# A spectral filter and a two-layer MLP in one kernel: the second inverse result is passed on through DRAM, with new planning costs

## The chip, the cores and the metric

One core of one Trainium2 chip runs the whole kernel. The metric is the device time of one execution in microseconds (us), of which a median over runs is shown. Engines are called as in the profile: PE (TensorE's matrix products), PEld (its weight loads), DVE (VectorE), ACT (ScalarE), POOL (GpSimd) and SP (SyncE, which issues every DMA of this kernel).

## What is computed

The reference, cut to its two halves (8 sequences of 3136 tokens with 256 channels):

```python
X = np.fft.rfft(x, axis=1)                       # along the tokens
y = np.fft.irfft(X * (filt_r + 1j * filt_i), n=3136, axis=1)
mixed = np.real(np.fft.fft(np.fft.fft(y, axis=1), axis=2))
u = y + mixed
un = (u - mean(u)) / sqrt(var(u) + 1e-6)         # over the channels
out = u + maximum(un @ w_ch1, 0) @ w_ch2         # 256 -> 1024 -> 256
```

## The kernel before, in words

**Stages of one sequence (batch b).** Every transform is a product with a constant matrix, each number split in two halves of 16 bits, so that three products replace one in 32 bits. `first` (L541) makes the first step of the transform from `x` and stores it to a DRAM tensor `d1` (L551); `load_at` brings it back in another order as seven tiles `at` (L574); `spectrum` (L615) makes the second step and multiplies with the filter on DVE and POOL; a transposing DMA gives `z` (L660); `inverse1` (L729) goes back one step and stores to the DRAM tensor `d2` (L743); `load_b2` brings that back as tiles `b2` (L772); `inverse2` (L791) makes the last step, and ACT puts its result into tiles `ys` (L804). One `ys` tile holds 224 token pairs: 2 halves of 56 partitions, 4 columns j, 256 channels.

**From `ys` to the MLP.** The MLP works on groups g of 256 token pairs (49 groups in all), in tiles `y_g` of 128 partitions by 2 halves t by 2 kinds. A `ys` tile does not fall on such tiles: `place` (L751 to L762) cuts it at the borders and copies each piece from SBUF to SBUF (L761), 632 DMAs in all. `prepare` waits until all pieces of its group have been placed, mixes the channels on PE (L851), adds on DVE (L861), and takes the mean and variance (L939, L940, ACT L943). `normalize` then makes `un` (ACT L968), the upper half `u16` (ACT L973) and the lower one (POOL L979), and transposes them with a DMA into `ut` (L982), two of them per group. There are two `ut` buffers and five `y` buffers.

**The MLP.** `products` goes through steps q: step 8g+f computes block f of the first product of group g (L1004, six matmuls from `ut`), and two steps later its part of the second product (L1047, twelve matmuls from `h`, into two PSUM tiles `acc`, one per half t). Between them `rectify` takes `h` out of PSUM on ACT (L1033) and DVE (L1035). After block 7, `finish` adds the sums to `y` on DVE (L1061) and `store` writes the rows out (L1067).

**What sets the order.** Nothing in the order is made at run time. `Plan` plays all tasks through with one queue per engine; a task names an engine and a length (`yield "PE", 1.31`), and the instructions are written down in the order in which the plan serves them. Each engine executes its list in that order and waits at each instruction for its semaphores. `gate(t)` lets a task begin only after step t has been planned; `FIRST` is the step, relative to 8g, at which `prepare(g)` may begin, and `COME` the one for `inverse2`. For SP the plan used one hold per issue, whatever the transfer:

```python
if e == "SP":
    self.free_at[e] = self.now + ISSUE
    self.moved = max(self.moved, self.now + ISSUE + REACH) + length
    self.end = self.moved + LANDED
```

`free_at` is when SP can issue again, `moved` when the DMA engines will have moved the bytes, `end` when a reader may start.

The functions that the diff touches follow, with the line numbers of the profile.

Of the kernel before, what the change touches and what calls it, by code (L numbers as in the profile page):

```python
# [10 lines left out]
F32 = mybir.dt.float32  # L11
# [15 lines left out]
NS = N // 2  # L27
# [2 lines left out]
EXPO = 0x7F800000  # L30
LAG = 2
YBUFS = 5
FIRST = -11
COME = 15
PIECE = 1.15
HALF = 1.45
# [2 lines left out]
POOL_SPLITS = (2,)  # L39
RAW_IN = ("ys", "ys", "b2", "ut", "ut", "ys", "b2", "ys")  # L40
RAW_AFTER = (6, 7, 8, 9, 10, 17, 18, 15)
ISSUE = 0.45
REACH = 0.8
LANDED = 1.5
HOP = 0.4

# [11 lines left out]
class Plan:  # L58
# [75 lines left out]
    def run(self):  # L134
        while self.heap:
            self.now, _, f, args = heapq.heappop(self.heap)
            f(*args)
            while self.heap and self.heap[0][0] <= self.now:
                _, _, f, args = heapq.heappop(self.heap)
                f(*args)  # L140
            for e, queue in self.queues.items():
                if queue and self.free_at[e] <= self.now:
                    _, _, task, length = heapq.heappop(queue)
                    if e == "SP":
                        self.free_at[e] = self.now + ISSUE
                        self.moved = max(self.moved, self.now + ISSUE + REACH) + length
                        self.end = self.moved + LANDED
                    else:
                        self.end = self.free_at[e] = self.now + length
                    self.post(self.free_at[e], int)  # L150
                    self.step(task, None, self.free_at[e] if e == "SP" else None)
        assert not self.live
# [141 lines left out]
def _program(ctx, tc, nc, a, NB):  # L294
# [188 lines left out]
    def load_x(b, t):  # L483
        yield gate(t)
        if b == 1:
            yield until(("placed", 0, 1, 1))
        ms[b] = tp.tile([112, 8], F32, tag="mx", name=f"mx_{b}")
        for q in range(7):
            yield gate(t + 1.2 * q)
            yield until(("own", "x", b, q))  # L490
            yield "SP", 1.6, t + 1.2 * q
            nc.sync.dma_start(xs[b, q], a["x"][b, :, 4 * q : 4 * q + 4])
            done("x", b, q)
# [18 lines left out]
    def first(b, q, t):  # L512
# [23 lines left out]
            give("big", 21 * b + q // 2)  # L536
        kp = yield take("psf")
        p = bank(f"s1_{b}_{q}")[:112].rearrange("p (n c) -> p n c", c=256)
        yield "PE", 0.74
        for i, (hs, hx) in enumerate(((0, 0), (0, 1), (1, 0))):  # L540
            nc.tensor.matmul(p, s1[:, hs], x16[:, hx], start=i == 0, stop=i == 2)  # L541
        give("x16", k)
# [175 lines left out]
    def inverse1(b, ch, h, t):  # L718
# [8 lines left out]
        yield "PE", 0.74  # L727
# [17 lines left out]
        done("d2", b, ch, h)  # L745

    backs = {}

    y_at = {}

    def place(ys, r, n, j, kind, slot):  # L751

        while n:
            tile_, p = divmod(slot, 128)
            m = min(n, 128 - p)
            g = tile_ // 2
            if g not in ys_of:
                y_at[g] = yield take("y")
                ys_of[g] = mp.tile([128, 2, 2, 256], F32, tag="y", name=f"y_{g}", bufs=YBUFS)
            yield "SP", 0.2  # L760
            nc.sync.dma_start(ys_of[g][p : p + m, tile_ % 2, kind], ys[r : r + m, j])  # L761
            r, n, slot = r + m, n - m, slot + m  # L762

    def load_b2(b):
        yield until(*(("d2", b, ch, h) for ch in range(7) for h in range(2)))
# [36 lines left out]
    def bring(b, c, o, ys, ky, kp, p):  # L802
        yield "ACT", 0.63
        nc.scalar.activation(ys[:, 2 * o : 2 * o + 2], p, AF.Copy, scale=alphas[b][:, 2:3])  # L804
        give("psf", kp)
        if o:
            yield until(("placed", b, c, 0))
        for j in (2 * o, 2 * o + 1):
            slot = b * NS + 224 * c + 56 * j
            for h in range(2):  # L810
                if c or j:
                    yield from place(ys, 64 * h, 56, j, h, slot)
                else:
                    for kind in range(2):
                        yield from place(ys, 64 * h + 28 * kind, 28, j, kind, slot + 28 * h)
        done("placed", b, c, o)
        if o:
            give("ys", ky)


    total = NB * NS
# [7 lines left out]
    def gate(t):  # L829
        return until(("step", int(t))) if t >= 0 else until()  # L830
# [55 lines left out]
    def pieces(g, size):  # L886
        lo, hi = 256 * g, 256 * g + 256
        return [
            (b, c) for b in range(NB) for c in range(NS // size)
            if b * NS + size * c < hi and b * NS + size * c + size > lo  # L890
        ]

    def prepare(g):
        yield gate(8 * g + FIRST)
        yield until(*(("eo", b, c) for b, c in pieces(g, 224)), *((("i2",),) if g == 0 else ()))
        yield until(*(("placed", b, c // 2, c % 2) for b, c in pieces(g, 112)))
        tiles = [(256 * g + 128 * t, 256 * g + 128 * t + 128) for t in range(2)]
        y = ys_of.pop(g)
        fix = None
# [90 lines left out]
    def products():  # L990
        yield until(("w1",))
        for q in range(8 * ng + LAG):
            g, f = divmod(q, 8)
            if g < ng:
                yield until(("ut", g, 0), ("ut", g, 1))
                kp = yield take("psh")
                p = spare(f"h_{g}_{f}")
                yield "PE", 1.31, q
# [17 lines left out]
            if q >= LAG:  # L1016
                g, f = divmod(q - LAG, 8)
                yield until(("h", g, f), *((("w2",),) if q == LAG else ()))
                if f == 0:
                    accs[g] = []  # L1020
                    for t in range(2):
                        k = yield take("pso")
                        accs[g].append((k, ps_o.tile([128, 2, 256], F32, tag="pso", name=f"acc_{g}_{t}")))
                yield "PE", 1.32, q + 0.5
                second_product(g, f)
                if f == 7:
                    plan.spawn(finish(g), q - 1000)

    def rectify(g, f, p, kp):
        k = yield take("h")  # L1030
# [6 lines left out]
        hs[g, f] = k, h  # L1037
        done("h", g, f)

    def second_product(g, f):  # L1040
        k, h = hs.pop((g, f))
        c0 = 0
        for t in range(2):
            acc = accs[g][t][1]
            for kind in range(2):
                for i, (hh, hw) in enumerate(((0, 0), (0, 1), (1, 0))):
                    nc.tensor.matmul(  # L1047
                        acc[:, kind],
                        h[:, hh, c0 : c0 + 128],
                        w2s[:, f, hw],  # L1050
                        start=f == 0 and kind == 0 and i == 0,
                        stop=f == 7 and kind == 1 and i == 2,
                    )
                c0 += 128
        give("h", k)

    def finish(g):
        y = ready[g][0]
        for t, (k, acc) in enumerate(accs.pop(g)):
            yield "DVE", 0.7  # L1060
            nc.vector.scalar_tensor_tensor(y[:, t], acc, beta, y[:, t], op0=ALU.mult, op1=ALU.add)  # L1061
            give("pso", k)
            plan.spawn(store(g, t, y), 8 * g + 14)

    def store(g, t, y):
        yield "SP", 0.8
# [121 lines left out]
    for b in range(NB):  # L1188
# [19 lines left out]
        plan.spawn(load_b2(b), brought(b, 0))  # L1208
        plan.spawn(inverse2(b), brought(b, 0))
    for g in range(ng):  # L1210
        plan.spawn(prepare(g), 8 * g + FIRST)
    plan.spawn(products(), 0)
    with tc.manual_schedule():
# [55 lines left out]
```

## Time and profile before

| | us |
|---|---|
| runs without profile (3) | 1633.46 median, 1633.34 to 1637.3 |
| the profiled execution | 1631.1 |
| its span, first to last instruction | 1629.3 |
| PE busy in the span | 1401.4 (86%) |
| DVE / ACT / POOL busy | 1125.9 / 779.1 / 541.6 |
| mean granted TensorE clock | 0.933 of full speed |
| share of the 16 DMA engines' time (queue q1) | 64.6% |

The busy time of PE contains matmuls that ran while the granted clock was halved, so it is no measure of work alone. The first 190 us of the span contain no MLP step: there batch 0 is transformed and the weights are split. SP's time is not counted as busy by the profile; how long an issue holds it stands in the view of one line's instructions.

### The profile page before, as it was taken

Reading aid. Unit: us, or ns where it says so; the run is one execution under the profiler, and the core shown is the slowest. Engines: PE = TensorE matmul, PEld = TensorE weight load, DVE = VectorE, ACT = ScalarE, POOL = GpSimd, SP = SyncE. Lnnn points to the kernel's source line nnn. Section 1 sums busy time; section 2 is a strip of 40 time slices with the busy share of each in tenths; the row PEclk is TensorE's granted clock in tenths of the full one; section 3 lists DMA queues with packets and bytes.
Section 4 is the critical chain, followed back from the end, with each engine's and each line's share of the span. In section 5 each row is a group of like instructions: output and inputs, shape, how many; then the busy total and the mean of one; then the engine's idle time right before and its main releaser. Section 6 shows DMA issues by size and latency. Waiting matters only on the chain.

```text
span 1629.3 us, 30652 instructions
## 1 busy us (share of the span) xinstructions
PE 1401.4 (86%) x11217; PEld 947.2 (58%) x11217; DVE 1125.9 (69%) x2409; ACT 779.1 (48%) x1450; POOL 541.6 (33%) x675
## 2 busy tenths in 40 slices
PE   3341799988899989999889998899898998999999
PEld 1240366655665556656566566666565665666666
DVE  6784977776668657677567867687666866654662
ACT  4452745463544634364454545464554634534432
POOL 4460166201850155311660047301760056301100
PEclk9555699998999989999999999999999999999999
DMA  7985497646885486837866487847886596533321
GB/s 212 219 209 163 110 194 166 179 127 158 174 184 136 123 189 156 190 103 165 160 152 186 114 178 157 194 135 164 158 171 155 142 182 145 150 87 83 87 74 45
DMA packets 412071, 247.48 MB, mean 152 GB/s; under 512 B 238832, under 2 KB 365856, under 8 KB 411920
## 3 DMA queue, kind: packets, MB, share of 16 engines
q1 hardware_dynamic: 411920, 245.52, 64.6%
q8 instruction: 88, 1.44, 0.4%
q14 instruction: 63, 0.52, 0.1%
HBM read 87.62 MB, written 77.07 MB: 101 GB/s over the span
## 4 chain that ended last, share of the span: by engine, by line
PE 32%; DMA 8%; DVE 5%; SPq 4%; POOL 4%; issue 2%; ACT 1%; DVEq 0%; ACTq 0%; POOLq 0%
PE h L1004 13%; PE acc L1047 13%; DMA b<-d 3%; SPq L761 2%; DMA ut<-u 2%; DVE y L861 2%; PE y L791 2%; SPq L574 1%; PE s L541 1%; DVE h L1035 1%; POOL y L656 1%; PE mix L851 1%; DMA x<-x 1%; DMA y<-ys 1%; DMA z<-y 1%
## 5 line engine op out<-in xcount | busy, mean ns | idle before, releaser
L1004 PE MATMUL h<-ut,w1s 128*128 128x512 f16 x2352 | 586.9, 386 | 51.8 <-DMA ut<-u 46.6
L1047 PE MATMUL acc<-w2s,h 128*128 128x256 f16 x4704 | 590.4, 276 | 16.8 <-DVE y L1061 16.8
L1047 PEld LDWEIGHTS <-h 128*128 128x128 f16 x4704 | 460.7, 99 | 158.3 <-issue 28.1
L1033 ACT ACTIVATE h<-h 128x512 f16<-128x512 f32 x392 | 233.1, 595 | 551.8 <-PE h L1004 547.1
L1035 DVE SCALAR_TENSOR_TENSOR h<-h,h 128x512 f16<-128x512 f32 x392 | 268.0, 684 | 264.4 <-ACT h L1033 263.2
L1004 PEld LDWEIGHTS <-w1s 128*128 128x128 f16 x2352 | 225.9, 99 | 266.1 <-issue 44.4
L979 POOL TENSOR_TENSOR u<-un,u 128x512 f16<-128x512 f32 x94 | 109.1, 1161 | 642.2 <-ACT u L973 546.6
L861 DVE SCALAR_TENSOR_TENSOR y<-mix,alpha,y 128x508 f32<-128x508 f32 (+1 forms) x368 | 162.1, 478 | 33.4 <-PE mix L851 15.7
L641 POOL TENSOR_TENSOR yt<-yt,t 128x224 f32<-128x224 f32 x105 | 70.0, 667 | 209.9 <-DVE yt L633 143.7
L968 ACT ACTIVATE un<-y,sb 128x256 f32<-128x256 f32 x196 | 111.3, 596 | 23.7 <-DVE sb L955 22.7
L656 POOL TENSOR_TENSOR y<-yt,y 128x448 f16<-128x448 f32 x105 | 108.5, 1036 | 34.5 <-ACT y L650 34.3
L541 PE MATMUL s<-x,s 112*112 112x512 f16 x336 | 98.9, 418 | 17.1 <-ACT x L530 8.8
L740 DVE TENSOR_TENSOR bt<-i,bt 112x512 f16<-112x512 f32 x112 | 75.3, 685 | 35.9 <-ACT bt L738 32.2
L384 DVE TENSOR_REDUCE mx<-x 112x1 f32<-112x1024 f32 x56 | 67.6, 1214 | 41.7 <-DMA x<-x 41.5
L729 PE MATMUL i<-z,i 112*112 112x256 f16 x224 | 66.1, 295 | 31.4 <-DMA z<-y 27.8
L738 ACT CAST bt<-i 112x512 f16<-112x512 f32 x112 | 64.6, 584 | 56.6 <-PE i L731 51.1
L532 DVE SCALAR_TENSOR_TENSOR x<-x,sx,x 112x512 f16<-112x512 f32 x111 | 86.5, 800 | 5.2 <-ACT x L530 5.1
L627 DVE TENSOR_TENSOR yt<-s,ft 128x448 f32<-128x448 f32 x112 | 69.0, 616 | 30.4 <-PE s L616 30.0
L615 PE MATMUL s<-s,at 112*128 112x56 f16 x896 | 65.5, 194 | 27.9 <-DMA at<-d 23.9
L791 PE MATMUL y<-b,i 112*64 112x512 f16 (+1 forms) x480 | 63.3, 387 | 30.3 <-DMA b<-d 30.3
L804 ACT ACTIVATE ys<-y,alpha 128x512 f32<-128x512 f32 x112 | 72.6, 685 | 33.9 <-PE y L791 20.6
L548 DVE TENSOR_TENSOR ast<-s,ast 112x512 f16<-112x512 f32 x112 | 75.0, 683 | 18.7 <-ACT ast L546 18.5
(130 smaller groups left out, 1620.8 us busy)
## 6 DMA issues: line engine op xcount, KB each, us to landing
x<-x SPq DMA_DIRECT2D x56, 448.0 KB
d<-ast SPq DMA_DIRECT2D x112, 224.0 KB
at<-d SPq DMA_DIRECT2D x56, 448.0 KB
d<-bt SPq DMA_DIRECT2D x112, 224.0 KB
b<-d SPq DMA_DIRECT2D x56, 448.0 KB
out<-y SPq DMA_DIRECT2D x98, 256.0 KB
y<-ys SPq DMA_DIRECT2D x268, 56.0 KB
raw<-w SPq DMA_DIRECT2D x8, 512.0 KB
```

The source lines that it names most:

```text
L532: nc.vector.scalar_tensor_tensor(x16[:, 1], x, sx[:112, 1:2], x16[:, 0], op0=ALU.mult, op1=ALU.subtract)
L541: nc.tensor.matmul(p, s1[:, hs], x16[:, hx], start=i == 0, stop=i == 2)
L656: nc.gpsimd.tensor_tensor(y16[:, :, 1, :112], ytv, y16[:, :, 0, :112], op=ALU.subtract)
L740: nc.vector.tensor_tensor(bt[:, :, 1], p, bt[:, :, 0], op=ALU.subtract)
L791: nc.tensor.matmul(p[64 * h : 64 * h + 64, js], i2[:, i_, h, i], bt[:, 2 * o + js.start : 2 * o + js.stop, h], start=i == 0, stop=i == 1,)
L861: nc.vector.scalar_tensor_tensor(out, p, al, y, op0=ALU.mult, op1=ALU.add)
L968: nc.scalar.activation(un[:, k], y[:, t, k], AF.Identity, bias=sb[:, i, 1:2], scale=sb[:, i, 3:4])
L979: nc.gpsimd.tensor_tensor(u16[:, :, :, 1], unv, u16[:, :, :, 0], op=ALU.subtract)
L1004: nc.tensor.matmul(p.rearrange("p (t k q) -> p t k q", t=2, k=2), w1s[:, d, hw, 128 * f : 128 * f + 128], utv[:, :, :, d, hx], start=i == ...
L1033: nc.scalar.activation(h[:, 0], p, AF.Relu)
L1035: nc.vector.scalar_tensor_tensor(h[:, 1], p, 0.0, h[:, 0], op0=ALU.max, op1=ALU.subtract)
L1047: nc.tensor.matmul(acc[:, kind], h[:, hh, c0 : c0 + 128], w2s[:, f, hw], start=f == 0 and kind == 0 and i == 0, stop=f == 7 and kind == 1 ...
```

## The change

Three things move together.

- `bring` no longer copies pieces to the `y` tiles. It stores each `ys` tile, when both of its halves are there, to a DRAM tensor `dy` of its batch with two DMAs of 56 partitions by 4 columns (six DMAs for the first tile of a batch). A new task `fetch(g)` loads the `y` tile of a group from `dy`, 128 rows per DMA (more, smaller ones where a batch ends inside a tile). `prepare` waits for `fetch`.
- The plan's costs: SP is held 1.4 us by a transposing DMA (`TURN`; those have the length 1.65) and 0.5 by any other, and it is held longer when the planned DMA work is more than 4.5 us ahead (`BACKLOG`). `REACH` falls from 0.8 to 0.5. Three PE lengths fall (0.74 to 0.66 for `first` and `inverse1`, 1.31 to 1.3 for the first product). `FIRST` is -13, and `fetch` may begin three steps before that.
- `second_product` and `finish` are served by half t, so that other PE work can be planned between the halves, and the sums of half 0 can be taken out before half 1 is computed.

```diff
-FIRST = -11
+FIRST = -13
-ISSUE = 0.45
-REACH = 0.8
+ISSUE = 0.5
+TURN = 1.4
+BACKLOG = 4.5
+REACH = 0.5
...
                     if e == "SP":
-                        self.free_at[e] = self.now + ISSUE
-                        self.moved = max(self.moved, self.now + ISSUE + REACH) + length
+                        issue = TURN if length == 1.65 else ISSUE
+                        self.moved = max(self.moved, self.now + issue + REACH) + length
+                        self.free_at[e] = max(self.now + issue, self.moved - BACKLOG)
...
     def load_x(b, t):
         if b == 1:
-            yield until(("placed", 0, 1, 1))
+            yield until(("placed", 0, 1))
...
+        done("ys", b, c, o)
         if o:
-            yield until(("placed", b, c, 0))
-        for j in (2 * o, 2 * o + 1):
-            slot = b * NS + 224 * c + 56 * j
+            yield until(("ys", b, c, 0))
+            if c == 0:
+                dys[b] = dp.tile([NS, 2, 256], F32, tag="dy", name=f"dy_{b}", bufs=3)
+            rows = dys[b][224 * c : 224 * c + 224].rearrange("(j q) k c -> k q j c", j=4)
             for h in range(2):
-                if c or j:
-                    yield from place(ys, 64 * h, 56, j, h, slot)
+                j = int(c == 0)
+                yield "SP", 0.7
+                nc.sync.dma_start(rows[h, :, j:], ys[64 * h : 64 * h + 56, j:])
...
+    def fetch(g):
+        yield gate(8 * g + FIRST - 3)
+        y_at[g] = yield take("y")
+        y = ys_of[g] = mp.tile([128, 2, 2, 256], F32, tag="y", name=f"y_{g}", bufs=YBUFS)
+        yield until(*(("placed", b, c) for b, c in pieces(g, 224)))
+        for t in range(2):
+            q, g1 = 256 * g + 128 * t, 256 * g + 128 * t + 128
+            while q < g1:
+                b = q // NS
+                e = min(g1, (b + 1) * NS)
+                p = q % 128
+                yield "SP", 1.6 * (e - q) / 256
+                nc.sync.dma_start(y[p : p + e - q, t], dys[b][q - b * NS : e - b * NS])
+                q = e
+        done("y", g)
...
-        yield until(*(("placed", b, c // 2, c % 2) for b, c in pieces(g, 112)))
+        yield until(("y", g))
...
-                if f == 0:
-                    accs[g] = []
-                    for t in range(2):
+                for t in range(2):
+                    if f == 0:
                         k = yield take("pso")
...
-                yield "PE", 1.32, q + 0.5
-                second_product(g, f)
-                if f == 7:
-                    plan.spawn(finish(g), q - 1000)
+                    yield "PE", 0.655, q + 0.5
+                    second_product(g, f, t)
+                    if f == 7:
+                        plan.spawn(finish(g, t), q - 1000)
```

**Where instructions move.** Three places, as the order of instructions lists them: the line of the program, the operation, what it writes and from what, and its size. Names end in a buffer number.

Before, on SP, between the two transposes of group 6; the first one stands four rows ahead of this piece. `y_7` and `y_8` are the tiles of later groups, `ast` is a tile of `first` of batch 2.

```order
L761 DMA y_8_3717<-ys_1_2_3663 8x256
L761 DMA y_8_3717<-ys_1_2_3663 48x256
L761 DMA y_8_3717<-ys_1_2_3663 8x256
L761 DMA y_8_3717<-ys_1_2_3663 56x256 x2
L551 DMA d1_2_3409<-ast_2_8_3746 112x1024
L761 DMA y_7_3671<-ys_1_1_3630 16x256
L761 DMA y_7_3671<-ys_1_1_3630 40x256
L761 DMA y_7_3671<-ys_1_1_3630 16x256
L761 DMA y_7_3671<-ys_1_1_3630 40x256
L761 DMA y_7_3671<-ys_1_1_3630 56x256 x2
L551 DMA d1_2_3409<-ast_2_9_3791 112x1024
L982 DMA_TRANSPOSE ut_6_3680<-u16_6_1_3776 128x8x128
```

Changed, the same place, with both transposes of group 6:

```order
L803 DMA dy_1_3284<-ys_1_1_3581 56x4x256 x2
L554 DMA d1_2_3360<-ast_2_6_3542 112x1024
L803 DMA dy_1_3284<-ys_1_2_3645 56x4x256 x2
L991 DMA_TRANSPOSE ut_6_3663<-u16_6_0_3694 128x8x128
L554 DMA d1_2_3360<-ast_2_7_3697 112x1024
L760 DMA b2_1_3_3734<-d2_1_1947 112x8x256
L825 DMA y_7_3416<-dy_1_3284 128x512 x2
L991 DMA_TRANSPOSE ut_6_3663<-u16_6_1_3730 128x8x128
```

Twelve copies and several stores between the two transposes have become two loads of `y_7`, one `b2` load and one store; the four stores of `ys` tiles stand ahead of both.

Before, on ACT, around the cast of the second half of group 9 (`u16_9_1`); `h16_8_k` is the rectified block k of the group ahead of it, so it counts the steps.

```order
L968 ACTIVATE un_9_1_4766<-y_9_3997,sb_9_4712 128x256
L1033 ACTIVATE h16_8_1_4785<-h_8_1_4770 128x512
L968 ACTIVATE un_9_1_4766<-y_9_3997,sb_9_4712 128x256
L650 CAST y16_2_106<-yt_2_3_4572 128x4x112
L738 CAST bt_2_2_0_4819<-i1_2_2_0_4784 112x2x256
L804 ACTIVATE ys_1_5_4786<-y_1_5_0_4811,alpha_1_1333 128x512
L973 CAST u16_9_1_4826<-un_9_1_4766 128x4x128
L738 CAST bt_2_2_1_4859<-i1_2_2_1_4824 112x2x256
L804 ACTIVATE ys_1_5_4786<-y_1_5_1_4855,alpha_1_1333 128x512
L650 CAST y16_3_107<-yt_2_3_4572 128x4x112
L650 CAST y16_0_104<-yt_2_4_4748 128x4x112
L1033 ACTIVATE h16_8_2_4885<-h_8_2_4847 128x512
```

Changed, the same cast:

```order
L1041 ACTIVATE h16_8_4_4831<-h_8_4_4809 128x512
L977 ACTIVATE un_9_0_4827<-y_9_4135,sb_9_4778 128x256
L982 CAST u16_9_0_4871<-un_9_0_4827 128x4x128
L741 CAST bt_2_2_1_4853<-i1_2_2_1_4839 112x2x256
L977 ACTIVATE un_9_1_4828<-y_9_4135,sb_9_4778 128x256 x2
L982 CAST u16_9_1_4907<-un_9_1_4828 128x4x128
L1041 ACTIVATE h16_8_5_4899<-h_8_5_4886 128x512
```

The cast stood between blocks 1 and 2 of group 8 and now stands between blocks 4 and 5, three steps nearer to the product that needs it.

Before, on SP, where batch 5 brings its `at` tiles; `b2_4_3` is an input of `inverse2` of batch 4.

```order
L574 DMA at_5_1_10715<-d1_5_10630 112x8x256
L574 DMA at_5_2_10768<-d1_5_10630 112x8x256
L574 DMA at_5_3_10971<-d1_5_10630 112x8x256
L574 DMA at_5_4_11017<-d1_5_10630 112x8x256
L772 DMA b2_4_3_11400<-d2_4_9191 112x8x256
L574 DMA at_5_5_11100<-d1_5_10630 112x8x256
```

Changed, the same place:

```order
L760 DMA b2_4_3_11169<-d2_4_9029 112x8x256
L577 DMA at_5_0_10524<-d1_5_10488 112x8x256
L577 DMA at_5_1_10552<-d1_5_10488 112x8x256
L577 DMA at_5_2_10595<-d1_5_10488 112x8x256
L577 DMA at_5_3_10824<-d1_5_10488 112x8x256
L577 DMA at_5_4_10846<-d1_5_10488 112x8x256
```

The load of `b2_4_3` has moved from behind five `at` loads to ahead of all of them.

## Rows read from the trace of the kernel before

**Rows 1.** Stretches: us, busy us of each engine (count), PE clock, DMA share, GB/s

```profile
204.00:1420.00 1216.00, 1114.40 (x9211) 757.79 (x9210) 872.03 (x1891) 600.08 (x1114) 452.75 (x574) 0.97 0.70 160
1420.00:1629.30 209.30, 201.31 (x1470) 134.55 (x1467) 106.90 (x243) 77.44 (x142) 18.50 (x16) 0.99 0.32 77
```

**Rows 2.** Waits of PE, 204 to 1420 us: who for whom, us in total, times, longest

```profile
PE h L1004 <- DMA ut<-u: 45.7, 13, 8.0
PE acc L1047 <- DVE y L1061: 16.8, 11, 5.0
PE i L729 <- DMA z<-y: 12.9, 7, 7.7
PE s L615 <- DMA at<-d: 12.2, 7, 5.2
PE y L791 <- DMA b<-d: 9.8, 8, 2.8
```

**Rows 3.** SP's holds by line: count, ns least/median/most, first and last start

```profile
L761 SPq DMA_DIRECT2D y<-ys x632: 532/746/1729, 129.4 to 1573.3; - x158
...
L982 SPq DMA_TRANSPOSE ut<-u x98: 1232/1283/4143, 181.5 to 1590.6; - x98
...
L1067 SPq DMA_DIRECT2D out<-y x98: 332/376/3047, 224.1 to 1626.1; - x98
```

**Rows 4.** Timeline of SP, group 6: start us, us held, line, operation, count

```profile
355.50 1.27 SPq L982 DMA_TRANSPOSE ut<-u  x1
...
357.93 4.24 SPq L761 DMA_DIRECT2D y<-ys  x6
...
362.79 4.32 SPq L761 DMA_DIRECT2D y<-ys  x6
...
367.79 1.32 SPq L982 DMA_TRANSPOSE ut<-u  x1
```

**Rows 5.** Timeline of POOL and PE, group 6; in brackets idle time and its end

```profile
354.85 1.16 POOL L979 TENSOR_TENSOR u<-un,u 128x512 f16<-128x512 f32 x1 [2.90 <-issue]
...
371.33 1.01 PE L1004 MATMUL h<-ut,w1s 128*128 128x512 f16 x2 [7.96 <-DMA ut<-u]
```

**Rows 6.** Stretch behind that wait: columns as in the first group

```profile
371.00:378.00 7.00, 6.67 (x24) 3.36 (x24) 2.89 (x8) 1.21 (x2) 0.00 (x0) 0.55 0.38 115
```

**Rows 7.** Timeline of POOL, SP and PE, group 11

```profile
511.18 1.15 POOL L979 TENSOR_TENSOR u<-un,u 128x512 f16<-128x512 f32 x1 [1.18 <-issue]
...
510.73 2.86 SPq L982 DMA_TRANSPOSE ut<-u  x2
...
516.98 1.46 PE L1004 MATMUL h<-ut,w1s 128*128 128x512 f16 x6
```

**Rows 8.** Timelines of DVE and PE, group 34: a wait for the sums

```profile
1233.55 1.22 DVE L384 TENSOR_REDUCE mx<-x 112x1 f32<-112x1024 f32 x1 [4.84 <-DMA x<-x]
...
1239.63 2.72 PE L1047 MATMUL acc<-w2s,h 128*128 128x256 f16 x12 [4.96 <-DVE y L1061]
```

**Rows 9.** Timelines of SP and PE before the first product

```profile
129.38 9.38 SPq L761 DMA_DIRECT2D y<-ys  x12
...
139.39 8.55 SPq L761 DMA_DIRECT2D y<-ys  x12
...
149.16 3.70 SPq L492 DMA_DIRECT2D x<-x  x7
...
163.93 0.37 PE L361 MATMUL pt_w<-ident,mw 128*1 128x128 f32 x1 [19.15 <-ACT mw L1138]
```

**Rows 10.** Chain that ended last: start us, us, what (DMA: issue to landing)

```profile
746.42 1.92 DMA y<-ys
757.22 3.47 DMA d<-ast
...
766.32 10.16 DMA b<-d
...
1061.78 4.11 DMA b<-d
```

**Rows 11.** Page, DMA queue: packets, MB, share of 16 engines' span

```profile
q1 hardware_dynamic: 411920, 245.52, 64.6%
```

More of the change, by code (lines that the diff above doesn't have):

```diff
@@ L538, in first @@
         p = bank(f"s1_{b}_{q}")[:112].rearrange("p (n c) -> p n c", c=256)
-        yield "PE", 0.74
+        yield "PE", 0.66
         for i, (hs, hx) in enumerate(((0, 0), (0, 1), (1, 0))):
@@ L726, in inverse1 @@
         p = bank(f"i1_{b}_{ch}_{h}")[:112].rearrange("p (j c) -> p j c", j=2)
-        yield "PE", 0.74
+        yield "PE", 0.66
         for i in range(2):
@@ L747, in _program @@
     backs = {}
[L749 to L762, printed above, removed]
     def load_b2(b):
@@ L805, in bring @@
         give("psf", kp)
+        done("ys", b, c, o)
         if o:
-            yield until(("placed", b, c, 0))
-        for j in (2 * o, 2 * o + 1):
-            slot = b * NS + 224 * c + 56 * j
+            yield until(("ys", b, c, 0))
+            if c == 0:
+                dys[b] = dp.tile([NS, 2, 256], F32, tag="dy", name=f"dy_{b}", bufs=3)
+            rows = dys[b][224 * c : 224 * c + 224].rearrange("(j q) k c -> k q j c", j=4)
             for h in range(2):
-                if c or j:
-                    yield from place(ys, 64 * h, 56, j, h, slot)
-                else:
+                j = int(c == 0)
+                yield "SP", 0.7
+                nc.sync.dma_start(rows[h, :, j:], ys[64 * h : 64 * h + 56, j:])
+                if c == 0:
                     for kind in range(2):
-                        yield from place(ys, 64 * h + 28 * kind, 28, j, kind, slot + 28 * h)
-        done("placed", b, c, o)
-        if o:
+                        yield "SP", 0.1
+                        nc.sync.dma_start(rows[kind, 28 * h : 28 * h + 28, 0], ys[64 * h + 28 * kind : 64 * h + 28 * kind + 28, 0])
             give("ys", ky)
+            done("placed", b, c)
+    dys, y_at = {}, {}
+    def fetch(g):
[13 more added lines that the diff above has]
+        done("y", g)
     total = NB * NS
@@ L997, in products @@
                 p = spare(f"h_{g}_{f}")
-                yield "PE", 1.31, q
+                yield "PE", 1.3, q
                 ut = ready[g][1]
@@ L1018, in products @@
                 yield until(("h", g, f), *((("w2",),) if q == LAG else ()))
-                if f == 0:
-                    accs[g] = []
-                    for t in range(2):
+                for t in range(2):
+                    if f == 0:
                         k = yield take("pso")
-                        accs[g].append((k, ps_o.tile([128, 2, 256], F32, tag="pso", name=f"acc_{g}_{t}")))
-                yield "PE", 1.32, q + 0.5
-                second_product(g, f)
-                if f == 7:
-                    plan.spawn(finish(g), q - 1000)
+                        accs[g, t] = k, ps_o.tile([128, 2, 256], F32, tag="pso", name=f"acc_{g}_{t}")
+                    yield "PE", 0.655, q + 0.5
+                    second_product(g, f, t)
+                    if f == 7:
+                        plan.spawn(finish(g, t), q - 1000)
     def rectify(g, f, p, kp):
@@ L1038, in rectify, with second_product, finish @@
         done("h", g, f)
[L1040 to L1057, printed above, removed]
-        y = ready[g][0]
[L1059 to L1063, printed above, removed]
+    def second_product(g, f, t):
+        k, h = hs[g, f]
+        acc = accs[g, t][1]
+        for kind in range(2):
+            c0 = 256 * t + 128 * kind
+            for i, (hh, hw) in enumerate(((0, 0), (0, 1), (1, 0))):
+                nc.tensor.matmul(
+                    acc[:, kind],
+                    h[:, hh, c0 : c0 + 128],
+                    w2s[:, f, hw],
+                    start=f == 0 and kind == 0 and i == 0,
+                    stop=f == 7 and kind == 1 and i == 2,
+                )
+        if t:
+            give("h", k)
+    def finish(g, t):
+        y = ready[g][0]
+        k, acc = accs.pop((g, t))
+        yield "DVE", 0.7
+        nc.vector.scalar_tensor_tensor(y[:, t], acc, beta, y[:, t], op0=ALU.mult, op1=ALU.add)
+        give("pso", k)
+        plan.spawn(store(g, t, y), 8 * g + 14)
     def store(g, t, y):
@@ L1210, in _program @@
     for g in range(ng):
+        plan.spawn(fetch(g), 8 * g + FIRST - 3)
         plan.spawn(prepare(g), 8 * g + FIRST)
```

## The prediction

> **What bounds the kernel now.** I read the stretches first, to see where PE is idle. From 204 to 1420 us PE is busy for 1114.40 of 1216 us and idle for 101.6; after 1420 only 8.0 are idle, so that end has nothing to give [rows 1]. The same row shows the second loss: a mean granted clock of 0.97. The rows at the lower of the two levels (1.2 against 2.4 GHz) lie behind waits: after the longest one, 8 us at 371, the clock of the next 7 us was 0.55, though PE was busy for 6.67 of them [rows 5, 6]. Three per cent of 1216 us are 36 us (30 to 43 by the rounding), or 0.35 us for each of the 101.6 idle ones. I price an idle microsecond of that stretch at 1.35.
>
> Next the waits say what ended the idle time: 45.7 us in 13 waits for `ut`, the transposed input of the first product; 16.8 for the sums that DVE must take out; 34.9 for the tiles `z`, `at` and `b` [rows 2]. None of these is PE's own work, so the question is why `ut` is late.
>
> The timeline answers it. In group 6 POOL finished the second `u` at 356.01 (354.85 + 1.16) [rows 5], and its transpose was issued at 367.79 [rows 4]: 11.8 us in which SP worked off what stood ahead, 8.56 of them holds of twelve `y` copies. The transpose took 3.54 us to the product (371.33 - 367.79). In group 11 POOL finished at 512.33, SP issued its second transpose within the 2.86 us that began at 510.73, and the product began at 516.98 without a wait [rows 7]. So the same chain meets its date when SP is free, and misses it when SP is not. SP is the resource in short supply, by its holds and not by the bytes: a `y` copy holds it 0.746 us, a transpose 1.283, while the plan booked 0.45 for either [rows 3].
>
> **The change part by part.**
>
> *SP's holds.* Removed: 632 copies x 0.746 = 471 us. Added: the order lists 144 stores (96 + 16 large, 32 small) and 104 loads. Neither exists before. Bounds: 0.376, the hold of a 256 KB store of `out`, and 0.746, the old copy, since the new stores also start on 56 partitions [rows 3]; 248 of them are 93 to 185 us. I take 0.376 for the loads, which have the shape of the `out` stores, and 0.746 for the stores: 39 + 107 = 146. SP gets 325 us back (286 to 378), 0.20 of the span.
>
> *Waits for `ut`.* The hold ahead of group 6's second transpose falls from twelve copies to two loads, a `b` load and one store. Against it speaks the order: the cast of group 9 moved three steps nearer to its product, and counted over groups 1 to 48 `prepare`'s mixing product stands 8.1 steps ahead of the first product, where it stood 8.9, in spite of the -13. The plan now books SP nearer to its true holds, so this lead is one that it can keep. I take three quarters of 45.7: 35 us (from 0 to 45.7; the loss side is a rival below).
>
> *Waits for the sums, 16.8.* Serving the halves apart lets `finish` of half 0 start earlier in the order. But the longest of these, 4.96 us, was DVE standing in front of an `x` load for 4.84 us, with `finish` queued behind it [rows 8]. That goes only if the load comes earlier. I take 6 (0 to 16.8).
>
> *Waits for `b`, 9.8, and for `at` and `z`, 25.1.* In batch 5 the `b2` load now stands ahead of seven `at` loads instead of behind five; one behind such loads took 10.16 us to land, one elsewhere 4.11 [rows 10]. The order shows this in four batches of seven. I take 3 for `b` and 4 for the others (0 to 12 together), since SP serves them too.
>
> *The clock.* 35 + 6 + 7 = 48 idle us, times 0.35: 17 us.
>
> *The start.* Before 164 us two runs of twelve copies hold SP for 9.38 and 8.55 us ahead of the seven `x` loads of batch 1 [rows 9]. Now eight stores stand there: 6.0 us at 0.746, so the loads can go 12 us earlier. On the other side the raw weights of the second product are loaded later in the new order, and PE waited 19.15 us for just those [rows 9]; but its transpose now stands behind nine blocks of `first` and three of the MLP. I take 8 (-5 to 12).
>
> *The detour.* A copy landed in 1.92 us; a store to DRAM took 3.47 and a load from it 4.11 to 10.16 [rows 10], so a tile comes 5.7 to 11.7 us later, and SP waits for the store before it issues the load: everything behind it in SP's list waits too, transposes included. Cover: `fetch` may start at step -16 and the mixing product stands at -8; a step is about 2.9 us (1.46 for a block of the first product [rows 7], as much for the second, which has as many columns), so 23 us. Without that cover the sum of DVE would stand still for each late tile. Bytes: 25.7 MB more on 245.52, 10.5%, which turns a DMA share of 0.70 into 0.77 in the main stretch [rows 1, 11]. I charge 8 us (0 to 40): a tenth on what is left of the waits for `at`, `z` and `b`, and a few late tiles.
>
> The shorter PE lengths and `REACH` only shape the order; no instruction of PE is added or dropped.
>
> **Sum.** 48 + 17 + 8 - 8 = 65 us off. Against the profiled execution's own time, 1631.1: 1566. The median of the runs shown is 1633.46, 2.4 above that execution; with the same distance I forecast **1568**.
>
> **A rule against this.** Where rows 4 show twelve holds of SP between a finished `u` and its transpose, the Trainium skill ("DMA: Bandwidth & Descriptors", "Issuing engines are not separate DMA queues") says that the time a sequencer spends on starting a DMA is usually small relative to the DMA itself. By that rule the 325 us would be worth next to nothing; this trace speaks against it, with 0.746 us of hold for a copy that lands in 1.92.
> The same page ("Anatomy of one DMA") warns of a "surprisingly long delay especially when the write target is HBM" before a DMA's completion is signalled. The trace agrees: 3.47 against 1.92 us [rows 10], and the price of the detour is worked out from those rows alone.
>
> **The rivals.**
>
> *A, the forecast:* `ut` waits mostly gone, 1568 (own range 1535 to 1600).
>
> *B, the DMA engines take over.* SP is freed, but the engines, at 0.70 on average, are full where a batch brings its `at` tiles. Waits for `at`, `z`, `b` (34.9) rise by 28, and only `ut` and the sums gain 41: net 13 x 1.35 = 18, start and detour cancel: 1615. For it: 10.16 us for one `b` load. Against it: the copies already moved half of those bytes.
>
> *C, slower: the lead is too short.* The chain from the mixing product to `ut` lost 0.9 step x 2.9 = 2.6 us of lead per group, and 13 groups of 48 have 7 steps or fewer (9 before). If SP's delay in front of the transposes falls by less than 2.6 us, for instance because SP now stands waiting for stores to land, the waits grow: 48 x 2.6 = 125 us of lost lead, of which I let half reach PE, as the rest had slack. 62 more and 13 saved elsewhere: 49 x 1.35 = 66: 1700. For it: the order of group 9. Against it: 11.8 us of delay in group 6, far above 2.6.
>
> *D, more than forecast.* With true holds the plan also cures `at`, `z` and the sums: three quarters of 101.6 idle us, 76 x 1.35 = 103: 1530. For it: all five waits pass through SP or DVE behind SP. Against it: `at` waits for bytes.
>
> *E, the rule above:* the holds don't matter; sums and `b` give 9 x 1.35 = 12, the detour takes 8: 1629, no change. Against it: group 11.
>
> **How the numbers follow.** A 0.57, B 0.12, C 0.10, D 0.15, E 0.06. A measurement of this kernel can tell about 0.3%, 5 us, from no change. Faster: A, D, B but for 0.02, and a sixth of E, 0.83; same 0.07; slower is C, 0.10. The range reaches from half of D's spread, 1515, to 1622, which takes in B; outside lie C, E and the end of D, near 0.2.
>
> **What would show it.** The wait list of PE from 204 to the end should show `ut` under 15 us; the holds of the new stores and loads should sum to 100 to 190 us; idle time of PE in the main stretch near 60 us and a clock of 0.98; `x` loads of batch 1 before 145 us. The forecast is wrong if `ut` stays above 35 us (C or E), if `at`, `z`, `b` pass 50 (B), or if DVE L870 waits for `y` tiles from DRAM by more than 20 us.

## The result and the profile after

The changed kernel takes 1522.15 us (median of four runs, 1520.26 to 1524.17) against 1634.68 for the kernel before in the same comparison (four runs, 1633.34 to 1637.3): a ratio of 0.931, 95% interval 0.9292 to 0.9328. The forecast was 1568 in a range of 1515 to 1622, faster at 0.83. The sign and the range held; the gain was 112 us where 65 were forecast, the size of rival D. Two runs stood far above the others of their kernel and are left out of every comparison here: one of experiment 2 (1680.39 us, at a mean clock of 0.824 where the others had 0.952 to 0.955) and one of the kernel before (5950 us).

The span of the profiled execution fell by 106.9 us (1629.3 to 1522.4). Where it came from is read from the stretch between the first product and the end, in the columns of [rows 1]. First the kernel before, then the changed one, whole and in the two parts that answer to [rows 1]:

```profile
189.50:1629.30 1439.80, 1330.21 (x10761) 900.57 (x10759) 991.54 (x2156) 690.61 (x1278) 471.24 (x590) 0.97 0.64 147
```

```profile
179.10:1522.40 1343.30, 1312.76 (x10769) 891.08 (x10769) 991.52 (x2177) 706.25 (x1298) 476.55 (x594) 0.99 0.77 177
...
190.00:1310.00 1120.00, 1096.78 (x9221) 749.60 (x9222) 868.96 (x1890) 615.16 (x1131) 457.01 (x577) 0.99 0.85 192
1310.00:1522.40 212.40, 206.09 (x1515) 137.77 (x1512) 112.04 (x266) 80.96 (x147) 19.54 (x17) 1.00 0.39 97
```

PE's idle time behind its first product went from 109.6 us (1439.80 - 1330.21) to 30.5: 79.1 us. The same matmuls took 17.4 us less, at a granted clock of 0.99 instead of 0.97. The first product begins 10.4 us earlier. 79.1 + 17.4 + 10.4 = 106.9, the whole difference of the spans. The main stretch has 23.2 idle us where it had 101.6, while the DMA engines' share rose from 0.70 to 0.85.

PE's waits from the first product to 1400 us, columns as in [rows 2]:

```profile
PE h L1013 <- DMA ut<-u: 11.6, 7, 3.6
PE acc L1054 <- DVE y L1068: 2.7, 6, 0.9
PE i L732 <- DMA z<-y: 1.9, 1, 1.9
PE h L1013 <- DVE y L870: 1.6, 1, 1.6
PE y L779 <- DMA b<-d: 0.2, 1, 0.2
```

Not `ut` alone but every wait of [rows 2] has fallen to about a quarter or less; the one for `at` no longer appears.

SP's holds by line, columns as in [rows 3]; the first three are the new stores and loads:

```profile
L803 SPq DMA_DIRECT2D dy<-ys x112: 325/404/1757, 126.5 to 1457.6; - x112
L825 SPq DMA_DIRECT2D y<-dy x104: 303/434/1255, 136.8 to 1462.9; - x104
L807 SPq DMA_DIRECT2D dy<-ys x32: 361/424/727, 126.9 to 1324.2; - x32
...
L991 SPq DMA_TRANSPOSE ut<-u x98: 1231/1308/5448, 174.2 to 1486.5; - x98
```

Summed over the trace the new ones hold SP for 121.2 us, where the 632 old copies held it for 457.9. All holds of SP together fell from 1085 to 783 us, in 981 issues instead of 1365.

The timelines of SP, POOL and PE in group 6, the place of [rows 4, 5]:

```profile
352.17 1.15 POOL L988 TENSOR_TENSOR u<-un,u 128x512 f16<-128x512 f32 x1 [0.97 <-POOL u L988]
...
353.93 0.38 SPq L760 DMA_DIRECT2D b<-d  x1
354.40 1.09 SPq L825 DMA_DIRECT2D y<-dy  x2
355.59 1.49 SPq L991 DMA_TRANSPOSE ut<-u  x1
...
361.56 1.69 PE L1013 MATMUL h<-ut,w1s 128*128 128x512 f16 x4 [2.05 <-DMA ut<-u]
```

POOL is done at 353.32, the transpose is issued at 355.59: 2.3 us where it was 11.8, and PE waits 2.05 where it waited 7.96. What is left of this wait is the transfer itself: 5.97 us from the issue to the product (361.56 - 355.59), where it took 3.54. Over all 98 transposes the median time from the end of the `u` to the issue fell from 3.5 to 0.28 us.

At the start, SP's timeline has the first of the seven `x` loads of batch 1 at 131.10 and the last at 140.92; in [rows 9] they begin at 149.16:

```profile
131.10 1.00 SPq L495 DMA_DIRECT2D x<-x  x1
133.08 0.36 SPq L1096 DMA_DIRECT2D raw<-w  x1
133.48 2.59 SPq L495 DMA_DIRECT2D x<-x  x5
136.81 2.14 SPq L825 DMA_DIRECT2D y<-dy  x2
140.92 0.33 SPq L495 DMA_DIRECT2D x<-x  x1
```

DVE's waits over the whole span, same columns as PE's:

```profile
DVE mx L387 <- DMA x<-x: 23.6, 18, 6.7
...
DVE y L870 <- DMA y<-dy: 2.1, 2, 1.6
```

Before, DVE waited 41.5 us for `x` and 13.7 for the `y` copies. For tiles from DRAM DVE waits 2.1 us.

### The profile page after: what moved, and what is told of

Same layout as the page of the kernel before. It is cut to its first block, busy times and chain, and to the rows that moved or that the text cites. A ratio compares the mean times of both kernels' runs of the same rounds, so it can differ in the third digit from the quotient of the medians.

```text
span 1522.4 us, 29999 instructions
## 1 busy us (share of the span) xinstructions
PE 1379.6 (91%) x11217; PEld 935.0 (61%) x11217; DVE 1114.9 (73%) x2409; ACT 784.4 (52%) x1450; POOL 541.5 (36%) x675
## 3 DMA queue, kind: packets, MB, share of 16 engines
q1 hardware_dynamic: 419680, 271.19, 77.0%
## 4 chain that ended last, share of the span: by engine, by line
PE 56%; DVE 4%; DMA 2%; issue 2%; ACT 1%; SPq 1%; POOL 1%; ACTq 0%; POOLq 0%; DVEq 0%
PE acc L1054 23%; PE h L1013 23%; PE y L779 3%; PE s L544 2%; PE mix L860 2%; DVE y L870 1%; PE i L732 1%; PE i L734 1%; PE i L733 1%; DMA ut<-u 1%; PE s L618 1%; PE s L619 1%; DMA b<-d 1%; DVE st L948 1%; DVE h L1043 1%
## 5 line engine op out<-in xcount | busy, mean ns | idle before, releaser
L1013 PE MATMUL h<-ut,w1s 128*128 128x512 f16 x2352 | 578.0, 382 | 16.1 <-DMA ut<-u 11.6
L1054 PEld LDWEIGHTS <-h 128*128 128x128 f16 x4704 | 452.0, 98 | 142.3 <-issue 18.8
L988 POOL TENSOR_TENSOR u<-un,u 128x512 f16<-128x512 f32 x94 | 109.6, 1167 | 598.4 <-ACT u L982 524.6
L977 ACT ACTIVATE un<-y,sb 128x256 f32<-128x256 f32 x196 | 110.7, 595 | 12.5 <-DVE sb L964 8.5
L659 POOL TENSOR_TENSOR y<-yt,y 128x448 f16<-128x448 f32 x105 | 109.6, 1048 | 18.7 <-ACT y L653 15.4
L551 DVE TENSOR_TENSOR ast<-s,ast 112x512 f16<-112x512 f32 x112 | 74.5, 684 | 15.3 <-ACT ast L549 14.9
L711 POOL TENSOR_TENSOR eo<-ef,eo 128x448 f16<-128x448 f32 (+6 forms) x62 | 59.7, 966 | 71.8 <-ACT eo L708 71.6
L387 DVE TENSOR_REDUCE mx<-x 112x1 f32<-112x1024 f32 x56 | 67.5, 1211 | 23.6 <-DMA x<-x 23.6
L948 DVE BATCH_NORM_STATS2 st<-y 128x6 f32<-128x256 f32 x196 | 80.8, 412 | 3.0
L544 PEld LDWEIGHTS <-s 112*112 112x112 f16 x336 | 46.3, 143 | 56.6 <-issue 37.1
```

The costliest lines, as they stand in the source:

```text
L659: nc.gpsimd.tensor_tensor(y16[:, :, 1, :112], ytv, y16[:, :, 0, :112], op=ALU.subtract)
L948: nc.vector.bn_stats(st[:, 2 * t + k], y[:, t, k])
L977: nc.scalar.activation(un[:, k], y[:, t, k], AF.Identity, bias=sb[:, i, 1:2], scale=sb[:, i, 3:4])
L988: nc.gpsimd.tensor_tensor(u16[:, :, :, 1], unv, u16[:, :, :, 0], op=ALU.subtract)
L1013: nc.tensor.matmul(p.rearrange("p (t k q) -> p t k q", t=2, k=2), w1s[:, d, hw, 128 * f : 128 * f + 128], utv[:, :, :, d, hx], start=i == ...
L1054: nc.tensor.matmul(acc[:, kind], h[:, hh, c0 : c0 + 128], w2s[:, f, hw], start=f == 0 and kind == 0 and i == 0, stop=f == 7 and kind == 1 ...
```

## The experiments

The change has three parts, and its gain two explanations. **H**: SP's holds made everything late that passes through its list, and the way through DRAM takes 302 us of them away. **P**: the plan's new costs put the work into a better order. Later expectations weigh two more. **R**: the way through DRAM gains by something other than SP's time. **U**: DMAs that the plan does not know of hurt only because they are not booked. The ratios below are to the kernel before on the same chip, which stood at 1630.0 to 1630.2 us in all three comparisons.

**1. The new costs alone.** The kernel before with the changed kernel's planning costs; copies, `FIRST` and whole products stay. (A `y` buffer is asked for once per group by a flag.)

```diff
-ISSUE = 0.45
-REACH = 0.8
+ISSUE = 0.5
+TURN = 1.4
+BACKLOG = 4.5
+REACH = 0.5
...
+                        issue = TURN if length == 1.65 else ISSUE
...
+                        self.free_at[e] = max(self.now + issue, self.moved - BACKLOG)
...
```

> The kernel before with the new planning costs alone (a transpose holds SP 1.4 us in the plan, another issue 0.5, backlog, REACH 0.5, the PE lengths); the copies from ys to y, FIRST -11 and the second product in one piece stay as they were. Theory H (SP's time is what was short, and the copies' holds are what takes it): 632 copies still hold SP for over 440 us, so PE's waits for ut from 204 us to 1420 stay over 25 us, and the time is 1600 to 1630. Theory P (SP had time enough, and the plan did not know its true holds): the waits for ut fall under 15 us and the time is 1540 to 1575.

Measured: 1624.73 us, 0.996 (0.9939 to 0.998). PE's waits from its first product on:

```profile
PE h L1010 <- DMA ut<-u: 49.7, 18, 6.9
PE y L797 <- DMA b<-d: 13.1, 8, 3.7
PE i L732 <- DMA z<-y: 11.1, 9, 3.8
```

The waits for `ut` stand as they were (46.6 us before), and SP's holds sum to 1089 us. P falls for this kernel: the new costs are worth 0.4% by themselves.

**2. The way through DRAM alone.** The kernel before with `dy`, `fetch` and the loads, as in the change's diff; costs, `FIRST` and whole products are the old ones.

```diff
-                    yield from place(ys, 64 * h, 56, j, h, slot)
...
+                nc.sync.dma_start(rows[h, :, j:], ys[64 * h : 64 * h + 56, j:])
...
+        plan.spawn(fetch(g), 8 * g + FIRST - 3)
```

> The kernel before with the way through DRAM alone (dy stores and fetch); old planning costs, FIRST -11, second product in one piece. H: SP's holds in all fall by about 300 us, waits for ut fall under 20 us, the time is 1545 to 1585. P: the plan still books a transpose at 0.45 us and keeps misplacing it, waits for ut stay over 25 us, the time is 1590 to 1630.

Measured: 1521.13 us (three runs), 0.9341 (0.9319 to 0.9363): the changed kernel's time, and below the range that H was given (1545 to 1585). PE's waits, from the first product to 1400 us, and the same stretch as above:

```profile
PE h L1010 <- DMA ut<-u: 8.0, 6, 2.9
PE acc L1053 <- DVE y L1067: 7.9, 8, 1.4
PE y L776 <- DMA b<-d: 2.3, 2, 1.5
PE s L615 <- DMA at<-d: 0.9, 1, 0.9
PE i L729 <- DMA z<-y: 0.9, 1, 0.9
```

```profile
181.50:1519.30 1337.80, 1304.01 (x10767) 888.35 (x10765) 991.77 (x2164) 699.84 (x1294) 475.15 (x594) 0.99 0.77 177
```

One part carries the whole gain: 75.8 of the 109.6 idle us go, and 26.2 us of PE's busy time. SP's holds sum to 783 us, as in the changed kernel.

**3 and 12. The changed kernel with the old costs**, taken twice.

```diff
-ISSUE = 0.5
-TURN = 1.4
-BACKLOG = 4.5
-REACH = 0.5
+ISSUE = 0.45
+REACH = 0.8
...
```

> The changed kernel with the old planning costs put back (way through DRAM, halves and FIRST -13 stay). H: close to the changed kernel, 1522 to 1550. P: most of the gain is lost, 1580 to 1630.

> The kernel of e3 once more, on the same chip as the two before it, for a comparison of less than one per cent: 1511 to 1517 by its four runs.

Measured: 1513.62 us, 0.9295 (0.9278 to 0.9312), and 1514.76, 0.9284 (0.9256 to 0.9311). Nothing is lost without the new costs; the time is even a little below H's 1522. The medians are the lowest of all kernels here, some 8 us below the changed kernel, but the intervals overlap with its 0.9292 to 0.9328: a better version, if at all, by half a per cent.

**4. The changed kernel with the copies back**, each planned at the new `ISSUE` of 0.5; costs, `FIRST` and halves as changed.

```diff
-                nc.sync.dma_start(rows[h, :, j:], ys[64 * h : 64 * h + 56, j:])
...
+                    yield from place(ys, 64 * h, 56, j, h, slot)
...
```

> The changed kernel with the copies from ys to y put back in place of the way through DRAM (new planning costs, halves and FIRST -13 stay; the plan books a copy at 0.5 us). H: SP is held for over 440 us by copies again, waits for ut over 25 us, 1590 to 1630. P: close to the changed kernel, 1525 to 1560.

Measured: 1613.28 us, 0.9912 (0.9877 to 0.9947). From the first product on:

```profile
PE h L1010 <- DMA ut<-u: 60.4, 20, 6.8
PE y L797 <- DMA b<-d: 8.2, 7, 2.2
...
PE s L618 <- DMA at<-d: 6.6, 4, 2.9
```

Without the way through DRAM the other two parts together are worth 0.9%. SP's holds are back at 1084 us.

**5. Idle issues.** Experiments 2 and 4 move SP's holds and the data's way together. This one separates them: experiment 3 plus 896 DMAs of 32 bytes each, eight behind each of 112 stores, into a DRAM tensor that nobody reads. The plan does not know of them, so the lists of all engines but SP are the same, row for row.

```diff
+                for i in range(8):
+                    r = 64 * h + 7 * i
+                    nc.sync.dma_start(dzs[b][c, 8 * h + i : 8 * h + i + 1], ys[r : r + 1, 1, :8])
```

> The kernel of e3 (way through DRAM, halves, FIRST -13, old planning costs) with 16 more DMAs behind each pair of dy stores, 896 in all: one row of 32 bytes each, from the same ys tile to a DRAM tensor that nothing reads. The plan is not told, so the order on every other engine is the same as in e3. H (SP's holds): at 0.30 to 0.40 us each SP gets back 270 to 360 us of holds, about what the copies took net; finished u tiles wait for SP again, PE's waits for ut rise from 8.8 to over 30 us and the time to 1570 to 1630. Rival R (it is not the holds but what the copies were: pieces between SBUF and SBUF that land late or burden the DMA engines): 29 KB in all burden nothing, the time stays at 1510 to 1530.

Measured: 1672.62 us, 1.0265 (1.023 to 1.0299), 159 us above experiment 3 and 43 beyond the end of H's range, though the idle issues hold SP for less than H expected (253 us instead of 270 to 360). First experiment 3, then this one: the stretch from the first product to the end.

```profile
186.20:1511.40 1325.20, 1301.94 (x10760) 886.14 (x10759) 987.27 (x2160) 695.34 (x1284) 471.80 (x591) 1.00 0.78 179
```

```profile
189.50:1665.90 1476.40, 1345.89 (x10760) 901.62 (x10759) 986.83 (x2160) 695.66 (x1284) 473.09 (x591) 0.96 0.69 160
```

PE has the same 10760 matmuls, 130.5 idle us instead of 23.3, and 44.0 us more of busy time at a clock of 0.96. What the idle DMAs hold SP for, and PE's waits:

```profile
L808 SPq DMA_DIRECT2D dz<-ys x896: 214/251/1518, 131.0 to 1607.3; - x180
```

```profile
PE h L1014 <- DMA ut<-u: 59.8, 20, 5.3
PE i L729 <- DMA z<-y: 25.4, 13, 4.3
PE s L615 <- DMA at<-d: 12.5, 7, 5.5
```

The 896 holds sum to 253.2 us and carry 29 KB. PE waits for none of these DMAs; what it waits for stands behind them. (The profile ends 53.4 us of POOL's idle time with one of them, as it ends 50.3 with a copy in the kernel before.) SP's and POOL's timelines in group 6:

```profile
360.86 1.16 POOL L989 TENSOR_TENSOR u<-un,u 128x512 f16<-128x512 f32 x1 [22.36 <-ACT u L983]
...
363.74 2.53 SPq L808 DMA_DIRECT2D dz<-ys  x8
366.31 0.32 SPq L801 DMA_DIRECT2D dy<-ys  x1
366.68 2.54 SPq L808 DMA_DIRECT2D dz<-ys  x8
369.33 1.24 SPq L992 DMA_TRANSPOSE ut<-u  x1
```

and the same place in experiment 3:

```profile
345.21 1.16 POOL L985 TENSOR_TENSOR u<-un,u 128x512 f16<-128x512 f32 x1 [21.77 <-ACT u L979]
...
346.40 1.24 SPq L988 DMA_TRANSPOSE ut<-u  x1
```

With them a finished `u` (362.02) waits 7.3 us for its transpose's issue, without them 0.03 (346.37 to 346.40). R falls: the way through DRAM is still there, and the gain is gone. The waits for `at` and `z` come back as well, although the DMA engines are less busy (0.69 against 0.78).

Are the transfers issued late, or have they become slower? The 20 transposes that PE waits for here were issued 4.0 us (median) after their `u` was finished. Taking for each the smaller of this delay and PE's wait, the delays cover 49.4 of the 59.8 us; in the kernel before they cover 46.1 of 46.6. From issue to product these transposes took 4.3 us (median), before 3.9: the lateness lies mainly ahead of the issue.

**9. The same, booked.** Each idle DMA now holds the planned SP for 0.25 us.

```diff
+                        hold = ISSUE if length else 0.25
...
+                    yield "SP", 0.0
```

> The kernel of e5 (896 idle DMAs of 32 bytes) with each of them booked in the plan at 0.25 us of SP, what one was measured to hold it, so that the plan can put others between them and move everything else. Holds are as in e5, about 1006 us. If what hurts is the part of SP's holds that the plan does not know (theory U), most of the 159 us come back: 1520 to 1560. If the hold itself is what costs, whoever knows of it (H in its plain form), at most a third comes back: 1620 to 1670. Between them, 1560 to 1620, both count.

Measured: 1665.94 us, 1.0211 (1.0191 to 1.023). From the first product on:

```profile
PE h L1016 <- DMA ut<-u: 86.7, 26, 11.2
```

Booking them gives back 7 of 159 us. U falls for the idle DMAs: this plan, told of the holds, does not hide them.

**6. The copies with their true price.** Experiment 4 with a copy booked at 0.75 us instead of 0.5.

```diff
+COPY = 0.75
...
-                        issue = TURN if length == 1.65 else ISSUE
+                        issue = TURN if length == 1.65 else COPY if length == 0.2 else ISSUE
```

> The kernel of e4 (copies put back, new planning costs, halves, FIRST -13) with the copies booked at their measured hold of 0.75 us in the plan instead of 0.5. H: the holds are still there, and a plan that knows them can only trade one wait for another: 1580 to 1620. P in its last form (the plan was wrong about the copies only): waits for ut under 20 us, 1530 to 1565.

Measured: 1588.09 us, 0.9746 (0.9718 to 0.9773); 42.5 us of waits for `ut`, in 10 instead of 20 waits. Knowing the hold is worth 25 us where the copies stay, against the 91 that separate experiment 4 from the changed kernel. So P has a part, but only with the copies: 2.5% below the kernel before.

**7, 8 and 11. The smaller parts**, each undone on experiment 3: `FIRST` back at -11, the products and sums whole again (as before the change), and `FIRST` at -15.

```diff
-FIRST = -13
+FIRST = -11
```

> The kernel of e3 with FIRST -11 instead of -13 (fetch begins at -14). If the two steps are worth something, waits for ut rise from 8.8 us by 5 to 25 and the time is 1520 to 1545; if the chain has slack since SP is free, 1508 to 1519.

```diff
-                    second_product(g, f, t)
+                second_product(g, f)
```

> The kernel of e3 with the second product and its sums in one piece again. If the halves matter, waits of the second product for DVE rise from 1.5 to 5 to 10 us and the time is 1518 to 1530; if not, 1508 to 1517.

```diff
-FIRST = -13
+FIRST = -15
```

> The kernel of e3 with FIRST -15. -11 gave 1527, -13 1514. If the lead is still short, 1500 to 1510; if five y buffers or the order of DVE now bind, 1514 to 1530.

Measured: 1526.69 us, 0.937 (0.9343 to 0.9397); 1524.13, 0.9358 (0.9326 to 0.939); 1530.15, 0.9387 (0.9373 to 0.9401). Each is 10 to 17 us slower than experiment 3, so -13 is better than two steps to either side. But experiment 2 has both of the first two undone at once and stands at 1521.13: the parts do not add up, each new order has some microseconds of its own. In experiment 7 the waits for `ut` from 204 us on rise from 8.8 to 13.1 us, 4.3 where at least 5 were expected. In experiment 8 the wait for the sums is 10.0 us where experiment 3 has 1.5; that is what serving the halves apart removes.

**10. New costs up to the first MLP step, old ones behind it**, to join the early start of the one (first product at 179.06 us) with the main stretch of the other (186.25).

```diff
+                        if self.begun:
+                            self.free_at[e] = self.now + 0.45
+                            self.moved = max(self.moved, self.now + 0.45 + 0.8) + length
```

> A search for a better version: the kernel of e3, with the new planning costs of SP up to the first step of the MLP and the old ones from there on (PE lengths the old ones). The start of the changed kernel reached its first product 7 us earlier than e3 did (179.1 against 186.2), the rest took 18 us longer. If the two add up: 1504 to 1511; if the start only moves a wait: 1511 to 1520.

Measured: 1516.15 us, 0.9295 (0.9277 to 0.9313). The first product begins at 176.32, 10 us earlier than in experiment 3 and 6 earlier than in experiment 12, and the total gains nothing: what is gained at the start is lost behind it.

The runs that decide, side by side (idle: PE behind its first product; waits for `ut` from there on; `u` to transpose: the median from a finished `u` to the issue of its transpose; all in us; the kernel before took 1630 beside the experiments):

| kernel | time | idle | waits for `ut` | SP's holds | `u` to transpose |
|---|---|---|---|---|---|
| before | 1634.7 | 109.6 | 46.6 | 1085 | 3.5 |
| changed | 1522.2 | 30.5 | 11.6 | 783 | 0.28 |
| 1, costs alone | 1624.7 | 105.7 | 49.7 | 1089 | 2.8 |
| 2, DRAM alone | 1521.1 | 33.8 | 8.0 | 783 | 0.03 |
| 3, changed, old costs | 1513.6 | 23.3 | 12.2 | 796 | 0.26 |
| 4, all but DRAM | 1613.3 | 99.2 | 60.4 | 1084 | 1.9 |
| 5, 3 + idle issues | 1672.6 | 130.5 | 59.8 | 1006 | 4.1 |
| 9, 5 booked | 1665.9 | 135.5 | 86.7 | 1020 | 1.8 |

## Why the prediction was right in sign, and 46 us short

**What bounds the kernel: right.** SP was named as the resource in short supply, by its holds and not by the bytes. Experiment 5 shows it: idle issues alone, with 29 KB of data, undo the gain.

**SP's holds: 325 forecast, 302 summed over the trace.** The stores were taken at 0.746 us, the row of the old copy from the same partitions; they held SP for 0.404 (small ones 0.424). The loads were taken at 0.376 and held it for 0.434. The new ones come to 121 us (100 to 190 was the sign to look for); by these terms alone the fall is 336.7 (457.9 - 121.2). That it is smaller in all lies with the other issues, which hold SP 35 us longer now, most of it in the 98 `ut` transposes (165.8 us, they were 143.0).

**Waits for `ut`: right.** 35 forecast; 46.6 to 11.6 us is 35.0, below the 15 that was set as the sign. The reason beside it was wrong: "The plan now books SP nearer to its true holds, so this lead is one that it can keep" has no worth in the runs once the copies are gone (experiment 1: 0.4%; experiments 3 and 12: nothing lost without it). The -13 that stood beside it is worth some 13 us (experiment 7 against 3), 4.3 of them in these waits (from 204 us on).

**Waits for the sums, `b`, `at` and `z`: the step that failed.** 13 of 51.7 us were forecast to go; 46.9 went (the sums 14.1, the others 32.8). The prediction carried SP's freed time through to `ut`, and hardly to the other transfers of the same list. Two sentences carried the low price. One, that the wait behind the `x` load "goes only if the load comes earlier": true, and the loads did, DVE's waits for them fell from 41.5 to 23.6 us. With the way through DRAM alone the wait for the sums is 7.9 us instead of 16.8 (experiment 2); the halves take most of what is left (10.0 to 1.5, experiment 8 against 3).

The other sentence, in rival D, "`at` waits for bytes", was false. Experiment 2 has 0.9 us of it at a DMA share of 0.77, and experiment 5 brings back 12.5 us in 7 waits at 0.69 (before: 12.2 in 7). These transfers were issued late, like the `ut` transposes. From the end of the last `ast` of a batch to the issue of its first `at` load passed 6.4 to 14.9 us before (batches 1 to 7), 2.7 to 6.4 in the changed kernel, 2.8 to 5.9 in experiment 3 and 6.1 to 11.8 in experiment 5. The loads that PE then waited for were no slower: 4.6 to 5.8 us from the first one's issue to the first product before, 3.8 to 5.3 in experiment 5. For `z` the median from the finished lower half to its transpose's issue was 3.8 us before, 1.1 changed, 0.9 in experiment 2 and 4.6 in experiment 5. D's condition, that all five waits pass through SP or through DVE behind SP, was the true one, and its 1530 the right size; but the cure is fewer holds, not true holds in the plan.

**The clock: right in total, by luck.** 17 forecast, 17.4 measured, but for 79.1 idle us instead of 48: 0.22 per idle us, so a price too high met too few idle us. In experiments 2 and 3 it is 26.2/75.8 and 28.3/86.3, 0.35 and 0.33, close to the price that was used; why the changed kernel got back less is open.

**The start: 8 forecast, 10.4 measured**, with the `x` loads 18 us earlier (131.10 against 149.16) where 12 were forecast.

**The detour: 8 forecast as a loss.** No loss of this size is seen: DVE waits 2.1 us for tiles from DRAM (20 was the sign against), and POOL's idle time that ends with one of these transfers is 47.9 us, with the old copies it was 50.3. The cover that the prediction named was enough for that. One of its readings does not hold: 3.47 us for a store against 1.92 for a copy do not show that writes to DRAM land late. The chain they come from lists copies of 1.92, 1.96, 3.19 and 4.63 us and stores of 2.14, 2.44, 3.03, 3.47 and 4.74.

**Sum.** Forecast 48 + 17 + 8 - 8 = 65, measured 79.1 + 17.4 + 10.4 = 106.9. Of the 41.9 between them 31.1 are waits, 8 the detour, 2.8 clock and start. The other 4 of the 46 lie between the profiled execution and the median: it was 2.4 below the median before, and 2.0 above it after.

**The rivals.** B fails: the DMA share rose to 0.85 in the main stretch and the waits for `at`, `z` and `b` fell. C fails: SP's delay in front of the transposes fell by 3.2 us in the median, more than the 2.6 us of lead that were lost. E, the rule of the Trainium skill ("DMA: Bandwidth & Descriptors", "Issuing engines are not separate DMA queues") that the time to start a DMA is usually small beside the DMA itself, forecast no change. Experiment 5 contradicts what it would make of this kernel: 896 starts of 0.251 us, in the one list from which the transfers go that PE waits for, cost 159 us.

**Open.** The 253 us of idle holds cost 159 (experiment 3 to 5), and SP's 1006 us in experiment 5 are fewer than the 1085 of the kernel before, which is 42 us faster. So the sum of the holds alone does not set the time; where they stand may, or something else that each issue costs. Nor do the waits follow the median delay from kernel to kernel (experiment 9: 1.8 us of delay, 86.7 of waits; over the 26 transposes that PE waited for there it is 4.4). In experiment 4 the delays cover only 34.9 of the 60.4 us of waits for `ut`; the rest arose ahead of the finished `u` and was not traced further. The runs do not separate the number of issues from their length. Copies issued from another engine's queue were not tried. That the old costs are 8 us better than the new ones on top of the change is seen in medians, not beyond the intervals.

## What to carry to other kernels

Where several engines wait for different transfers that one queue issues, add up how long its issues hold that queue, and measure for one late transfer the time from its producer's end to its issue: a "wait for a DMA" may be a wait for the queue. Then fewer, larger issues can be worth more than fewer bytes or a shorter way: here 10% more bytes through DRAM took 7% off the time. To tell holds from bytes, add small idle issues and leave all else as it is.

## What the runs showed of the hardware

- The hold of an issue is not set by its bytes (medians): a copy of 56 KB or less between on-chip tiles held SP for 0.746 us, a store of mostly 224 KB from the same partitions 0.404, a 256 KB load 0.434, 32 bytes 0.251.
- With 0.85 of the DMA engines' time taken instead of 0.70, and 25.7 MB more on the queue (271.19 against 245.52), none of PE's waits for a transfer grew in the main stretch.
- PE's busy time for the same matmuls ran from 1301.94 us at a clock of 1.00 to 1345.89 at 0.96: the idle time that a late queue causes is paid a second time, in the clock of the matmuls behind it (0.55 in the 7 us behind the longest wait, [rows 6]).
